# P times V in plain float32, two heads side by side on TensorE's columns

## The chip, the cores and the metric

The kernel runs on one core of one Trainium2 chip. A core has TensorE (PE, matmuls from SBUF into PSUM), VectorE (DVE), ScalarE (ACT), GpSimd (POOL) and a queue of transfers issued by SyncE (SP). The metric is the device time of one execution in microseconds, the median of several runs.

## The reference

Three parts run one behind the other for 4 batches (B), 8 heads (H), 576 tokens (S) and a head size of 64 (D).

```python
scores = scale * np.matmul(q, k.transpose(0, 1, 3, 2))
cum = np.cumsum(np.maximum(s, 0.0), axis=-1)
bias = -(cum[:, :, :, None] - cum[:, :, None, :])
scores = np.where(causal, -1000000000.0, scores + np.minimum(bias, 0.0))
attn = softmax(scores)              # max, exp, sum, divide
x = np.matmul(attn, v)              # "P times V", heads side by side: [B, S, 512]
h = relu(x @ w_in); gate = sigmoid(conv3(h)); x = (h * gate) @ w_out
u = x + (x.T @ U @ V).T
out = u + relu(u @ w_ch1) @ w_ch2
```

The change is in `x = np.matmul(attn, v)`, and in a small part of `scores`.

## The kernel before, in words

The kernel is written as a list of operations, each with an engine, an estimated cost and what it reads and writes. A planner (`Plan.order`) issues them in a simulated order in time: on each engine the operation that is ready and was written first goes first. Eight PSUM banks are given out by class (`sc` for scores, `pt` for transposes, one at a time, `av` for P times V, and so on).

Attention runs over 32 heads, two heads being a pair that shares loads. `att_head(h)` (L1335) writes the scores and the softmax of head `h`, and the transposes and P times V of head `h - 1`. A head's 576 query rows are five blocks: `scores` (L700) makes one block of 128 rows against the keys that the causal mask leaves; `scores4` (L730) makes the last 64 rows of both heads of a pair in one bank, in two halves of 288 keys. DVE adds the mask and takes the maximum, ACT makes the exponentials, POOL divides. `transp` (L775) turns the blocks of P in four groups, and `av` (L809) multiplies: the first half is the queries 0 to 255 (group 0, two steps of widths 256 and 128), the second the queries 256 to 575 (groups 1 to 3, five steps of widths 320, 320, 320, 192 and 64). The steps of a half accumulate in one bank and so keep their order. Every width is a number of queries that stream past a block of 128 keys of V.

There are two forms of arithmetic. In the heads 0 to 7 (`FS` for the scores, `FV` for P times V) the operands are plain float32, and the trace shows two PE instructions for each such matmul. In the heads 8 to 31 each operand is split in a high and a low part of type fp32r (`hi_...` and `lo_...`, L352 to L365), and a product is built from one instruction for each pair of parts that counts. For P times V, V's high and low parts stand side by side in 128 columns (`vv`), P's high and low parts are two tiles (`th` from ACT, `tl` from DVE), and each step is two instructions. The bank then holds two halves of 64 partitions, which ACT and DVE add up (L854, L857).

The first MLP's weights are decoded and split while the first twelve heads run (`load_split`). Its matmuls for one batch (`m1_in` L882, `m1_out` L924) are written between the heads of the next batch, so from head 9 on they fill PE between the steps of attention. When attention ends, its pool in SBUF is closed and the last MLP's weights and activations are put in its place; the second MLP (`m2_in`, `m2_out`) follows.

Of the kernel before, what the change touches and what calls it, by code (L numbers as in the profile page):

```python
# [22 lines left out]
HS = S // 2  # L23
# [2 lines left out]
KT = DM // 128  # L26

FS = range(8)
FV = range(8)

CHUNKS = [512, 512, 512, 512, 256]

# [14 lines left out]

CAPS = dict(sc=3, pt=1, av=5, h=4, y=4, tp=2, t1=4, mh=1, ma=8, my=8, mx=2)

RINGS = dict(P=2, qk=2, th=3, vv=2, qkh=1, x=2, wf=2, xs=5, g=12, hh=3, c=3, x2=4, w64=2, mh=5, o=4, snap=2, tt=3)  # L50


def f32(ap):
# [256 lines left out]
def tile_attention_moe_mixer(  # L310
# [44 lines left out]
    def hi_pool(out, src, r, w, n):  # L355
        pool(n, lambda: nc.gpsimd.tensor_scalar(out(), src(), 1.0, 1.0, ALU.mult, ALU.mult), r, w)
# [230 lines left out]

    def prep_v(h):

        vr = ring(ap, "vr", 1, [128, 2, 5, 64], F32, f"vr{h}")  # L590
        dma(327680, lambda: nc.sync.dma_start(out=vr(), in_=vP[h // 2]), [], [vr])
        for o in range(2):
            if h + o in FV:
                st["v", h + o] = (vr, lambda j, o=o: vr[:, o, j, :])
                continue
            vv = ring(ap, "vv", RINGS["vv"], [128, 5, 128], F32R, f"vv{h + o}")
            hi_pool(lambda vv=vv: vv[:, :, 0:64], lambda o=o: vr[:, o], [vr], [(vv, 0)], 320)
            lo_pool(
                lambda vv=vv: vv[:, :, 64:128],
                lambda o=o: vr[:, o],  # L600
                lambda vv=vv: vv[:, :, 0:64],
                [vr, (vv, 0)],
                [(vv, 1)],
                320,
            )
            st["v", h + o] = (vv, lambda j, vv=vv: vv[:, j, :])

    def prep(h):

# [75 lines left out]
    def products(h, ps, rows, q0, k0, w):  # L685
# [11 lines left out]

        pe(16 + 1.88 * w if h in FS else 2 * mm(w, rows), mms, d["qk"], [ps])

    def scores(h, i):  # L700
        P, sm = st[h]["P"][i], st[h]["sm"]
        w = 128 * i + 128
        ps = bank("sc", f"sc{h}_{i}")
        products(h, ps, 128, 128 * i, 0, w)
        top(ps, 128, w, 384 - 128 * i, lambda: sm[:, i : i + 1], None, [], (sm, f"m{i}"))
        exps(
            lambda: P[:, :w],
            ps,
            128,
            w,  # L710
            lambda: sm[:, i : i + 1],
            lambda: sm[:, 4 + i : 5 + i],
            (sm, f"m{i}"),
            [P, (sm, f"s{i}")],
        )
        if i in RECIP:
            ns = range(max((x + 1 for x in RECIP if x < i), default=0), i + 1)
            ss = [(sm, f"s{n}") for n in ns]
            rs = [(sm, f"r{n}") for n in ns]

            def r():
                return sm[:, 8 + ns[0] : 9 + i]

            dve(2, lambda: nc.vector.tensor_scalar(r(), sm[:, 4 + ns[0] : 5 + i], 1e-9, None, ALU.add), ss, rs)
            dve(15, lambda: nc.vector.reciprocal(r(), r()), rs, rs)  # L725
            for n in ns:
                Pn = st[h]["P"][n]
                normalise(Pn, 128 * n + 128, lambda n=n: sm[:, 8 + n : 9 + n], (sm, f"r{n}"), [Pn])

    def scores4(h):  # L730

        P, sm = st[h]["P"][4], sm4s[h // 2 % 2]
        tiles = []
        for n in range(2):
            ps = bank("sc", f"sc{h}_4_{n}")

            products(h + 1, ps, 128, S - 128, n * HS, HS)
            products(h, ps, 64, S - 64, n * HS, HS)
            top(
                ps,  # L740
                128,
                HS,
                512 * n,
                lambda n=n: sm[:, n : n + 1],
                None if n == 0 else lambda: sm[:, 0:1],
                [] if n == 0 else [(sm, "m0")],
                (sm, f"m{n}"),
            )
            tiles.append(ps)
        for n, ps in enumerate(tiles):  # L750
# [18 lines left out]
        dve(15, lambda: nc.vector.reciprocal(sm[:, 4:5], sm[:, 4:5]), [(sm, "r")], [(sm, "r")])  # L769
        normalise(P, S, lambda: sm[:, 4:5], (sm, "r"), [(P, 0), (P, 1)])  # L770
# [4 lines left out]
    def transp(h, g):  # L775
        d = st[h]
        pt = bank("pt", f"pt{h}_{g}")
        blocks, pos, off, cost = [], {}, 0, 0
        for j, i0, i1 in GROUPS[g]:
            pos[j] = off  # L780
            for i in range(i0, i1 + 1):
                rows = 128 if i < 4 else 64
                blocks.append((j, i, rows, off))
                off += rows
                cost += 109
        n = off

        def tr():


            for j, i, rows, o in reversed(blocks):
                turn = ident[:, 128:256] if i == 4 and h % 2 == 0 else ident[:, 0:128]
                nc.tensor.transpose(
                    pt[:, o + rows - 128 : o + rows], d["P"][i][:, 128 * j : 128 * j + 128], turn
                )

        pe(cost, tr, [ident] + [d["P"][i] for i in sorted({b[1] for b in blocks})], [pt])
        if h in FV:
            th = ring(ap, "th", RINGS["th"], [128, 512], F32, f"tf{h}_{g}")
            hi_act(lambda: th[:, :n], lambda: pt[:, :n], [pt], [th], n)  # L800
            d[f"g{g}"] = ((th,), pos)
            return
        th = ring(ap, "th", RINGS["th"], [128, 512], F32R, f"th{h}_{g}")
        tl = ring(ap, "tl", RINGS["th"], [128, 512], F32R, f"tl{h}_{g}")
        hi_act(lambda: th[:, :n], lambda: pt[:, :n], [pt], [th], n)
        lo_dve(lambda: tl[:, :n], lambda: pt[:, :n], lambda: th[:, :n], [pt, th], [tl], n)
        d[f"g{g}"] = ((th, tl), pos)

    def av(h, half):  # L809
        d = st[h]  # L810
        b, hh = divmod(h, H)
        n, q0, g0 = (256, 0, 0) if half == 0 else (320, 256, 2)
        vb, vof = st["v", h]
# [6 lines left out]
        m = 64 if h in FV else 128  # L820
        tot = len(ops) * m // 64
        c = 0
        for _, g, j, o in ops:
            ts, pos = d[f"g{g}"]
            w = n - o

            def mms(c=c, j=j, o=o, ts=ts, at=pos[j], w=w):
                for k, t in enumerate(ts):
                    nc.tensor.matmul(
                        ps[:m, o:n],  # L830
                        lhsT=vof(j),
                        rhs=t[:, at : at + w],
                        start=c + k == 0,
                        stop=c + k == tot - 1,
                    )

            pe(max(4 * w / 2.4, 160) if h in FV else 2 * mm(w), mms, [vb, *ts], [ps])
            c += len(ts)
        dt = hh // 2
        if hh % 2 == 0 and half == 0:  # L840
            st["x", b, dt] = ring(ap, "x", RINGS["x"], [128, S], F32, f"x{b}_{dt}")
        x = st["x", b, dt]

        def xo():
            return x[a0 : a0 + 64, q0 : q0 + n]

        a0 = 64 * (hh % 2)
        b0 = 64 - a0
        key = (x, (hh % 2, half))
        if h in FV:  # L850
            act(n, lambda: nc.scalar.copy(xo(), ps[0:64, :n]), [ps], [key])
        else:
            tmp = ring(ap, "avt", 1, [128, 320], F32, f"avt{h}_{half}")
            act(n, lambda: nc.scalar.copy(tmp[a0 : a0 + 64, :n], ps[b0 : b0 + 64, :n]), [ps], [tmp])  # L854
            dve(
                n,
                lambda: nc.vector.tensor_tensor(  # L857
                    xo(), ps[a0 : a0 + 64, :n], tmp[a0 : a0 + 64, :n], ALU.add
                ),
                [ps, tmp],  # L860
                [key],
            )
        if hh % 2 == 1 and half == 1:
# [471 lines left out]
    def att_head(h):  # L1335
# [20 lines left out]
            scores(h, 2)  # L1356
        if h > 0:
            transp(h - 1, 1)
            av(h - 1, 0)
        if h < NH:  # L1360
            scores(h, 3)
        if h > 0:
# [1 line left out]
            transp(h - 1, 3)  # L1364
        if h < NH and h % 2 == 0:
            scores4(h)
        if h > 0:
            av(h - 1, 1)

    def mix_parts(b):  # L1370
        def begin():
# [223 lines left out]
```

## Time and profile before

| | |
|---|---|
| median of 3 runs | 849.58 us (849.27 to 849.73) |
| profiled execution, first to last instruction (span) | 847.6 us |
| what the median has beside that span | 2.0 us |
| PE busy | 813.4 us, 96% |
| DVE, ACT, POOL busy | 606.6, 471.0, 392.7 us |
| heads 0 to 7, first MLP weights | to about 77 us |
| heads 8 to 31 with the first MLP | about 77 to 378 us |
| rest of the first MLP, mixing, first layer of the second MLP | about 378 to 647 us |
| second layer of the second MLP | 647 us to the end |

The profiler gives the span of the execution that it took; the time of an execution as the runs measure it is somewhat more than such a span. Matmuls overlap in the records: one is listed for longer than the engine is kept from the next. So start to next start is what a matmul costs.

### The profile page before, as it was taken

To read this page: it belongs to the slowest core of one execution; us is meant where nothing else is said; L and a number is where in the kernel's file an instruction comes from. 1 tells how busy PE (TensorE), PEld (TensorE's weight loads), DVE (VectorE), ACT (ScalarE), POOL (GpSimd) and SP (SyncE) were. 2 spreads that over 40 slices of the span, in tenths; PEclk is the share of its full clock that TensorE was granted. 3 is DMA by queue.
4 is the path that set the end of the run, shared out by engine and by line. 5 is a ranking of instruction groups with operands and counts; after the bars stand their busy time and mean duration, and the time that the engine had idled before them with its cause. 6 is when DMAs were issued, how large, how long until landed. Compare 5 with 4: busy or idle time off the path is not lost. (4 is left out here: it accounts for less than half of the span.)

```text
span 847.6 us, 15619 instructions
## 1 busy us (share of the span) xinstructions
PE 813.4 (96%) x5300; PEld 736.0 (87%) x5300; DVE 606.6 (72%) x1326; ACT 471.0 (56%) x1176; POOL 392.7 (46%) x489
## 2 busy tenths in 40 slices
PE   5989999999999999999997999999999999999998
PEld 3555899999899999999997999999998888888888
DVE  6876999867997589967799989877588732323232
ACT  4887898867877588767675343433344422222211
POOL 3766875864456536447276667555465200000000
PEclk9999999999999999999999999999999999999999
DMA  6666753662455434402134444645368663545443
GB/s 181 185 169 181 197 118 107 161 163 59 129 145 129 115 82 127 129 25 84 56 106 136 156 145 135 205 155 168 128 215 261 194 185 111 176 118 164 127 124 100
DMA packets 66311, 119.71 MB, mean 141 GB/s; under 512 B 9396, under 2 KB 34868, under 8 KB 66232
## 3 DMA queue, kind: packets, MB, share of 16 engines
q1 hardware_dynamic: 66160, 118.70, 48.7%
q8 instruction: 42, 0.69, 0.3%
q14 instruction: 37, 0.30, 0.1%
q10 hardware_dynamic: 72, 0.01, 0.0%
HBM read 68.81 MB, written 28.90 MB: 115 GB/s over the span
## 5 line engine op out<-in xcount | busy, mean ns | idle before, releaser
L1277 PE MATMUL my<-mh,w 128*128 128x512 f32 (+1 forms) x560 | 158.8, 368 | 0.0
L1258 DVE SCALAR_TENSOR_TENSOR ml<-ml,mh 128x512 fp32r<-128x512 f32 (+1 forms) x80 | 53.2, 673 | 104.4 <-ACT mh L1255 104.4
L1178 PE MATMUL ma_S<-u,W 128*128 128x288 f32 x768 | 119.7, 296 | 5.0 <-DVE s L1194 4.9
L935 PE MATMUL y<-gh,w1o 128*128 128x288 f32 x512 | 118.0, 301 | 0.5 <-DVE c L914 0.5
L1255 ACT ACTIVATE mh<-ml 128x512 fp32r<-128x512 f32 (+1 forms) x80 | 46.9, 589 | 127.7 <-DMA ml<-ch_d 68.8
L1277 PEld LDWEIGHTS my<-mh,w 128*128 128x128 f32 x560 | 101.6, 189 | 17.5
L1178 PEld LDWEIGHTS ma_S<-u,W 128*128 128x128 f32 x768 | 107.5, 188 | 7.4 <-DVE s L1194 7.3
L679 POOL TENSOR_SCALAR P<-P,sm 128x128 f32<-128x128 f32 (+3 forms) x128 | 73.4, 592 | 82.6 <-DVE sm L725 76.6
L1277 PE MATMUL my<-ml,w 128*128 128x512 f32 (+1 forms) x280 | 103.0, 368 | 0.0
L1178 PE MATMUL ma_A<-u,W 128*128 128x288 f32 x576 | 92.8, 296 | 1.6 <-ACT p L1190 1.5
L935 PEld LDWEIGHTS y<-gh,w1o 128*128 128x128 f32 x512 | 86.3, 188 | 1.7 <-DVE c L914 1.1
L1178 PEld LDWEIGHTS ma_A<-u,W 128*128 128x128 f32 x576 | 81.9, 188 | 2.7 <-ACT p L1190 2.2
L365 POOL TENSOR_TENSOR gl<-c,gh 128x288 fp32r<-128x288 f32 x64 | 55.5, 870 | 61.8 <-ACT gh L920 58.5
L651 DVE CUSTOM_DVE_ANT_0 sc<-sc,mask 128x128 f32<-128x128 f32 (+2 forms) x144 | 68.6, 495 | 20.7 <-PE sc L690 19.3
L893 PE MATMUL h<-xh,w1h 128*128 128x290 f32 x256 | 80.0, 312 | 1.1 <-DVE c L914 0.7
L893 PE MATMUL h<-xl,w1h 128*128 128x290 f32 x256 | 76.2, 298 | 0.0
L893 PE MATMUL h<-xh,w1l 128*128 128x290 f32 x256 | 76.1, 297 | 0.0
L935 PE MATMUL y<-gl,w1o 128*128 128x288 f32 x256 | 75.0, 293 | 0.0
L668 ACT ACTIVATE P<-sc,sm 128x128 f32<-128x128 f32 (+3 forms) x128 | 67.6, 531 | 11.5 <-DVE sm L651 9.9
L905 DVE SCALAR_TENSOR_TENSOR c<-h,cw,c 128x288 f32<-128x288 f32 x128 | 64.1, 509 | 5.8 <-ACT c L901 4.9
L362 DVE TENSOR_TENSOR tl<-pt,th 128x384 fp32r<-128x384 f32 x96 | 54.5, 567 | 10.8 <-ACT th L353 10.6
L1277 PEld LDWEIGHTS my<-ml,w 128*128 128x128 f32 x280 | 52.8, 189 | 8.7
(147 smaller groups left out, 1989.6 us busy)
## 6 DMA issues: line engine op xcount, KB each, us to landing
ml<-ch_d SPq DMA_DIRECT2D x64, 256.0 KB
ch_d<-p SPq DMA_DIRECT2D x64, 144.0 KB
raw_w<-w_in SPq DMA_DIRECT2D x16, 512.0 KB
raw_w2a<-w_in SPq DMA_DIRECT2D x16, 512.0 KB
raw_w2b<-w_in SPq DMA_DIRECT2D x16, 512.0 KB
t<-qk_in SPq DMA_DIRECT2D x24, 288.0 KB
qkB<-t SPq DMA_DIRECT2D x24, 288.0 KB
qkA<-t SPq DMA_DIRECT2D x24, 288.0 KB
```

The costliest lines, as they stand in the source:

```text
L362: dve(n, lambda: nc.vector.tensor_tensor(out(), src(), f32(hi()), ALU.subtract), r, w)
L365: pool(n, lambda: nc.gpsimd.tensor_tensor(out(), src(), f32(hi()), ALU.subtract), r, w, two=True)
L651: lambda: nc.vector.tensor_tensor_reduce(out=ps[:rows, :w], in0=ps[:rows, :w], in1=mask[:rows, m0 : m0 + w], scale=-0.125, scalar=3.0e38 i ...
L668: lambda: nc.scalar.activation(out(), ps[:rows, :w], ACTF.Exp, bias=low(), scale=-1.0, accum_out=total()),
L679: lambda: nc.gpsimd.tensor_scalar(t[:, :w], t[:, :w], r(), 1.0, ALU.mult, ALU.mult),
L893: nc.tensor.matmul(ps[:, :W], lhsT=ww, rhs=xx, start=kt + n == 0, stop=kt == KT - 1 and n == 2)
L905: lambda k=k: nc.vector.scalar_tensor_tensor(c(), hh[:, k : k + HS], cw[:, 3 * f + k : 3 * f + k + 1], c(), ALU.mult, ALU.add),
L935: nc.tensor.matmul(ps[:, :HS], lhsT=ww, rhs=xx(), start=f + n == 0, stop=f == NF1 - 1 and n == 2)
L1178: nc.tensor.matmul(ps[:, :HS], lhsT=ww, rhs=uu, start=k == 0, stop=k == 5)
L1255: act(n, lambda: nc.scalar.activation(mh[:, :n], raw(), ACTF.Relu), [ml], [mh])
L1258: lambda: nc.vector.scalar_tensor_tensor(ml[:, :n], raw(), 0.0, f32(mh[:, :n]), ALU.max, ALU.subtract),
L1277: nc.tensor.matmul(ys[c][dt][:, :n], lhsT=ww, rhs=xx[:, :n], start=f + k == 0, stop=f == NF2 - 1 and k == 2)
```

## The change

P times V is done in plain float32 in all heads, not only in the first eight. Neither P nor V is split any more: `prep_v` only loads V, and `transp` makes one tile for each group, by ACT. `av` takes a pair of heads at once. One bank of 128 partitions holds both: each step is a float32 matmul of the even head on the array's columns 0-63 and one of the odd head on columns 64-127, written in turns. ACT copies both heads out in one instruction of 128 partitions, and DVE's addition is gone. `av` of a pair is written in the head after the pair's second. The tiles of transposed P have their own buffers for each group and for even and odd heads, and V has two buffers. In the first eight heads the last 64 rows of both heads of a pair are also made as two float32 products on columns 0-63 and 64-127 (`last_rows`).

```diff
-FV = range(8)
-RINGS = dict(P=2, qk=2, th=3, vv=2, ...)
+RINGS = dict(P=2, qk=2, vr=2, ...)
 def prep_v(h):
-        vr = ring(ap, "vr", 1, [128, 2, 5, 64], F32, f"vr{h}")
+        vr = ring(ap, "vr", RINGS["vr"], [128, 2, 5, 64], F32, f"vr{h}")
         dma(327680, lambda: nc.sync.dma_start(out=vr(), in_=vP[h // 2]), [], [vr])
-            hi_pool(lambda vv=vv: vv[:, :, 0:64], ...)
-            lo_pool(lambda vv=vv: vv[:, :, 64:128], ...)
+        st["v", h // 2] = vr
+    def last_rows(h, ps, k0, w):
+        ts = [st[h + o]["qk"][0] for o in range(2)]
+        def mms():
+            for o, t in enumerate(ts):
+                nc.tensor.matmul(
+                    ps[64 * o : 64 * o + 64, :w],
+                    lhsT=t[:, 0, S - 64 : S],
+                    rhs=t[:, 1, k0 : k0 + w],
+                    start=True, stop=True,
+                    tile_position=(0, 64 * o),
+                )
+        pe(16 + 2.7 * w, mms, ts, [ps])
 def scores4(h):
+            if h in FS:
+                last_rows(h, ps, n * HS, HS)
+            else:
                 products(h + 1, ps, 128, S - 128, n * HS, HS)
                 products(h, ps, 64, S - 64, n * HS, HS)
 def transp(h, g):
-        th = ring(ap, "th", RINGS["th"], [128, 512], F32R, f"th{h}_{g}")
-        tl = ring(ap, "tl", RINGS["th"], [128, 512], F32R, f"tl{h}_{g}")
+        th = ring(ap, f"th{h % 2}_{g}", 1 if h % 2 or g > 1 else 2, [128, n], F32, f"th{h}_{g}")
         hi_act(lambda: th[:, :n], lambda: pt[:, :n], [pt], [th], n)
-        lo_dve(lambda: tl[:, :n], lambda: pt[:, :n], lambda: th[:, :n], [pt, th], [tl], n)
 def av(h, half):
+            pairs = [st[h + e][f"g{g}"] for e in range(2)]
+            def mms(c=c, j=j, o=o, w=w, pairs=pairs):
+                for e, (t, pos) in enumerate(pairs):
+                    nc.tensor.matmul(
+                        ps[64 * e : 64 * e + 64, o:n],
+                        lhsT=vr[:, e, j, :],
+                        rhs=t[:, pos[j] : pos[j] + w],
+                        start=c == 0, stop=c == len(ops) - 1,
+                        tile_position=(0, 64 * e),
+                    )
-            pe(max(4 * w / 2.4, 160) if h in FV else 2 * mm(w), mms, [vb, *ts], [ps])
+            pe(max(4 * w / 2.4, 160), mms, [vr, *(t for t, _ in pairs)], [ps])
-            act(n, lambda: nc.scalar.copy(xo(), ps[0:64, :n]), [ps], [key])
-            act(n, lambda: nc.scalar.copy(tmp[a0 : a0 + 64, :n], ps[b0 : b0 + 64, :n]), [ps], [tmp])
-            dve(n, lambda: nc.vector.tensor_tensor(xo(), ps[...], tmp[...], ALU.add), [ps, tmp], [key])
+        act(n, lambda: nc.scalar.copy(x[:, q0 : q0 + n], ps[:, :n]), [ps], [(x, half)])
 def att_head(h):
-            av(h - 1, 0)
+            if h % 2 == 0:
+                av(h - 2, 0)
-        if h > 0:
-            av(h - 1, 1)
+        if h > 0 and h % 2 == 0:
+            av(h - 2, 1)
```

## Rows read from the trace of the kernel before

**Rows 1.** The page, part 1: busy time of each engine, share of the span, instructions.
```profile
PE 813.4 (96%) x5300; PEld 736.0 (87%) x5300; DVE 606.6 (72%) x1326; ACT 471.0 (56%) x1176; POOL 392.7 (46%) x489
```

**Rows 2.** Windows: stretch and length, busy time by engine, PE's clock, DMA share, GB/s.
```profile
17.80:77.30 59.50, 54.48 (x256) 31.60 (x256) 48.38 (x124) 47.35 (x127) 41.94 (x46) 1.00 0.61 172
77.30:378.00 300.70, 295.18 (x2171) 280.58 (x2170) 248.06 (x686) 236.89 (x656) 175.29 (x270) 1.00 0.49 123
```

**Rows 3.** Timeline of PE, a float32 head: start, length, instruction, count.
```profile
60.56 0.86 PE L829 MATMUL av<-tf,vr 128*64 128x256 f32 x4
61.35 0.33 PE L793 MATMUL pt<-ident,p 128*128 128x128 f32 x1
...
61.83 2.27 PE L829 MATMUL av<-tf,vr 128*64 128x320 f32 x10
64.03 0.44 PE L793 MATMUL pt<-ident,P 128*128 128x128 f32 x2
```

**Rows 4.** Timeline of PE, split heads: first and following instruction of three blocks.
```profile
148.49 0.31 PE L829 MATMUL av<-th,vv 128*128 128x320 f32 x1
148.64 0.31 PE L829 MATMUL av<-tl,vv 128*128 128x320 f32 x1
148.78 0.22 PE L690 MATMUL sc<-qkB 128*128 128x128 f32 x1
...
151.04 0.31 PE L829 MATMUL av<-th,vv 128*128 128x320 f32 x1
...
151.71 0.33 PE L793 MATMUL pt<-ident,P 128*128 128x128 f32 x1
...
154.12 0.28 PE L829 MATMUL av<-th,vv 128*128 128x256 f32 x1
...
154.41 0.28 PE L829 MATMUL av<-tl,vv 128*128 128x128 f32 x1
154.52 0.30 PE L690 MATMUL sc<-qkB 128*64 128x288 f32 x1
```

**Rows 5.** Timeline of PE where float32 and split matmuls meet.
```profile
39.06 0.70 PE L690 MATMUL sc<-qkF 128*128 128x256 f32 x2
39.53 0.40 PE L893 MATMUL h<-xh,w1h 128*128 128x290 f32 x1
39.77 0.30 PE L893 MATMUL h<-xl,w1h 128*128 128x290 f32 x1
39.91 0.29 PE L893 MATMUL h<-xh,w1l 128*128 128x290 f32 x1
40.13 0.86 PE L829 MATMUL av<-tf,vr 128*64 128x256 f32 x4
```

**Rows 6.** Timeline of PE, last rows of a float32 pair, then its P times V.
```profile
29.39 2.01 PE L690 MATMUL sc<-qkF 128*64 128x288 f32 x6
31.24 0.43 PE L829 MATMUL av<-tf,vr 128*64 128x320 f32 x1
```

**Rows 7.** Groups of instructions, whole run: count, busy us, mean ns, idle before.
```profile
L362 DVE TENSOR_TENSOR tl<-pt,th 128x384 fp32r<-128x384 f32 x96 | 54.5, 567 | 10.8 <-ACT th L353 10.6
...
L857 DVE TENSOR_TENSOR x<-av,avt 64x256 f32<-64x256 f32 (+1 forms) x48 | 21.7, 452 | 7.6 <-ACT avt L854 4.5 <-POOL xl L365 2.3
L365 POOL TENSOR_TENSOR vv<-vr,vv 128x320 fp32r<-128x320 f32 x24 | 21.5, 896 | 1.3
...
L854 ACT COPY avt<-av 64x256 f32<-64x256 f32 (+1 forms) x48 | 18.9, 394 | 3.9 <-PE av L829 2.9
...
L356 POOL TENSOR_SCALAR vv<-vr 128x320 fp32r<-128x320 f32 x24 | 13.4, 561 | 10.2 <-PE av L829 8.3 <-DMA vr<-vP_in 1.3 <-PE sc L690 0.6
...
L851 ACT COPY x<-av 64x256 f32<-64x256 f32 (+1 forms) x16 | 6.3, 393 | 0.9 <-PE av L829 0.7
```

**Rows 8.** Waits of PE and of its weight loads, 77 to 380 us: total, times, longest.
```profile
PE pt L793 <- ACT P L668: 2.0, 2, 1.0
...
PEld h L893 <- DVE c L914: 1.6, 4, 1.0
```

More of the change, by code (lines that the diff above doesn't have):

```diff
@@ L48 @@
 CAPS = dict(sc=3, pt=1, av=5, h=4, y=4, tp=2, t1=4, mh=1, ma=8, my=8, mx=2)
-RINGS = dict(P=2, qk=2, th=3, vv=2, qkh=1, x=2, wf=2, xs=5, g=12, hh=3, c=3, x2=4, w64=2, mh=5, o=4, snap=2, tt=3)
+RINGS = dict(P=2, qk=2, vr=2, qkh=1, x=2, wf=2, xs=5, g=12, hh=3, c=3, x2=4, w64=2, mh=5, o=4, snap=2, tt=3)
 def f32(ap):
@@ L588, in prep_v @@
     def prep_v(h):
-        vr = ring(ap, "vr", 1, [128, 2, 5, 64], F32, f"vr{h}")
+        vr = ring(ap, "vr", RINGS["vr"], [128, 2, 5, 64], F32, f"vr{h}")
         dma(327680, lambda: nc.sync.dma_start(out=vr(), in_=vP[h // 2]), [], [vr])
[L592 to L606, printed above, removed]
+        st["v", h // 2] = vr
     def prep(h):
@@ L698, in products @@
         pe(16 + 1.88 * w if h in FS else 2 * mm(w, rows), mms, d["qk"], [ps])
+    def last_rows(h, ps, k0, w):
[6 more added lines that the diff above has]
+                    rhs=t[:, 1, k0 : k0 + w],
+                    start=True,
+                    stop=True,
+                    tile_position=(0, 64 * o),
+                )
+        pe(16 + 2.7 * w, mms, ts, [ps])
     def scores(h, i):
@@ L735, in scores4 @@
             ps = bank("sc", f"sc{h}_4_{n}")
-            products(h + 1, ps, 128, S - 128, n * HS, HS)
-            products(h, ps, 64, S - 64, n * HS, HS)
+            if h in FS:
+                last_rows(h, ps, n * HS, HS)
+            else:
+                products(h + 1, ps, 128, S - 128, n * HS, HS)
+                products(h, ps, 64, S - 64, n * HS, HS)
             top(
@@ L797, in transp @@
         pe(cost, tr, [ident] + [d["P"][i] for i in sorted({b[1] for b in blocks})], [pt])
[L798 to L802, printed above, removed]
-        th = ring(ap, "th", RINGS["th"], [128, 512], F32R, f"th{h}_{g}")
-        tl = ring(ap, "tl", RINGS["th"], [128, 512], F32R, f"tl{h}_{g}")
+        th = ring(ap, f"th{h % 2}_{g}", 1 if h % 2 or g > 1 else 2, [128, n], F32, f"th{h}_{g}")
         hi_act(lambda: th[:, :n], lambda: pt[:, :n], [pt], [th], n)
-        lo_dve(lambda: tl[:, :n], lambda: pt[:, :n], lambda: th[:, :n], [pt, th], [tl], n)
-        d[f"g{g}"] = ((th, tl), pos)
+        d[f"g{g}"] = (th, pos)
     def av(h, half):
-        d = st[h]
-        b, hh = divmod(h, H)
+        b, dt = h // H, h % H // 2
         n, q0, g0 = (256, 0, 0) if half == 0 else (320, 256, 2)
-        vb, vof = st["v", h]
+        vr = st["v", h // 2]
         ps = bank("av", f"av{h}_{half}")
@@ L819, in av @@
         ops.sort()
[L820 to L824, printed above, removed]
+        for c, (_, g, j, o) in enumerate(ops):
             w = n - o
-            def mms(c=c, j=j, o=o, ts=ts, at=pos[j], w=w):
-                for k, t in enumerate(ts):
+            pairs = [st[h + e][f"g{g}"] for e in range(2)]
+            def mms(c=c, j=j, o=o, w=w, pairs=pairs):
+                for e, (t, pos) in enumerate(pairs):
@@ L829, in mms @@
                     nc.tensor.matmul(
[L830 to L834, printed above, removed]
-                    )
-            pe(max(4 * w / 2.4, 160) if h in FV else 2 * mm(w), mms, [vb, *ts], [ps])
-            c += len(ts)
-        dt = hh // 2
-        if hh % 2 == 0 and half == 0:
+                        ps[64 * e : 64 * e + 64, o:n],
@@ L841, in av @@
+                        lhsT=vr[:, e, j, :],
+                        rhs=t[:, pos[j] : pos[j] + w],
+                        start=c == 0,
+                        stop=c == len(ops) - 1,
+                        tile_position=(0, 64 * e),
+                    )
+            pe(max(4 * w / 2.4, 160), mms, [vr, *(t for t, _ in pairs)], [ps])
+        if half == 0:
             st["x", b, dt] = ring(ap, "x", RINGS["x"], [128, S], F32, f"x{b}_{dt}")
         x = st["x", b, dt]
-        def xo():
-            return x[a0 : a0 + 64, q0 : q0 + n]
@@ L847, in av @@
[L847 to L850, printed above, removed]
-            act(n, lambda: nc.scalar.copy(xo(), ps[0:64, :n]), [ps], [key])
-        else:
-            tmp = ring(ap, "avt", 1, [128, 320], F32, f"avt{h}_{half}")
-            act(n, lambda: nc.scalar.copy(tmp[a0 : a0 + 64, :n], ps[b0 : b0 + 64, :n]), [ps], [tmp])
[L855 to L862, printed above, removed]
@@ L863, in av @@
-        if hh % 2 == 1 and half == 1:
+        act(n, lambda: nc.scalar.copy(x[:, q0 : q0 + n], ps[:, :n]), [ps], [(x, half)])
+        if half == 1:
             th = ring(xp, "xh", RINGS["xs"], [128, S + 2], F32R, f"xh{b}_{dt}")
```

## The prediction

> **What bounds the kernel now.** I read the page's busy shares first, then the shares by stage, then the order on TensorE in two stages, then the waits. TensorE (PE) is busy for 96% of the span [rows 1], but that is a mean over stages of different work, so the table of stretches decides [rows 2]. The page's chain of waits starts only in the later stages and says nothing of the stage that changes.
>
> - Stage 1, heads 0 to 7 in float32 (17.8 to 77.3 us): PE is busy 54.5 of 59.5 us, but VectorE (DVE) 48.4 and ScalarE (ACT) 47.4. PE leads, with two engines close behind.
> - Stage 2, heads 8 to 31 between the first MLP's matmuls (77.3 to 378 us): PE 295.2 of 300.7 us, DVE 248.1, ACT 236.9, GpSimd (POOL) 175.3. PE is the bound, and 5.5 us is all that its waits hold.
> - The two stages behind it hold nothing of the change. They shift as a block: the space of the attention pool is handed on when attention ends.
>
> So in stage 2 the change is worth what it does to PE's own time; the work it takes from DVE, ACT and POOL is mostly off the path.
>
> **What a head's P times V costs on PE today.** Matmuls overlap in the records, so I take start to next start. In float32 [rows 3] the first half (widths 256 and 128, two instructions each) goes from 60.56 to 61.35, 0.79 us, and the second (320, 320, 320, 192, 64) from 61.83 to 64.03, 2.20 us: 2.99 us a head, 5.98 a pair. Each of the two instructions streams at two cycles of 2.4 GHz a column: 2 x 1600 columns x 2 / 2.4 GHz = 2.67 us, and the rest is the entry to each block. In split form [rows 4] the first half takes 154.12 to 154.52, 0.40; the first 320 148.49 to 148.78, 0.29; the second 320 the same by its form; the last three 151.04 to 151.71, 0.67. That is 1.65 a head, 3.30 a pair.
>
> **The new form.** A pair has seven steps, each of four instructions: head A first and second, head B first and second, A on columns 0-63 and B on 64-127. No row of before shows two matmuls side by side on different columns, so the price is bounded from both sides. With no overlap a pair costs its two heads, 5.98 us. With full overlap it costs one head, 2.99.
>
> I choose near the lower end. A float32 instruction of width 320 takes 0.27 us and a split one of the same width 0.15 [rows 3, 4], so two float32 streams side by side ask for about the data that one split stream already gets, and the halves share no columns and no weights. But starts follow program order in every row. So A's second instruction must start before B's first: A1 runs alone, A2 beside B1, then B2 beside the next step's A1. With T the time of one instruction, a step on its own costs 3T, and n steps in a row 2T each plus one T.
>
> The last steps, in one block: 0.27 + 2 x (3 x 0.267 + 0.16 + 0.053) = 2.29; the first half 0.213 + 2 x 0.32 = 0.85. Sum 3.15 a pair. Where the steps come apart as they do in stage 2 of before (the first half, 320, 320, then three together [rows 4]): 0.85 + 0.80 + 0.80 + 1.23 = 3.68.
>
> To this comes the change of form. In [rows 5] the last float32 scores go from 39.06 to 39.53 for 0.43 us of streaming; the first split matmul behind them then takes 0.24 to the next start and the second 0.14, so leaving float32 costs about 0.14; entering costs 0.08 (39.91 to 40.13 against 0.14). Behind a transpose the entry is paid today as well. I count 0.15 a block: two blocks 0.3, four 0.6.
>
> - Stage 2: a pair goes from 3.30 to between 3.45 and 4.28; twelve pairs, +1.8 to +11.8 us. Other work is always ready there to come between the steps, but steps behind transposes pay nothing extra for entry, so I take +0.45 a pair, **+5.4 us**.
> - Stage 1, P times V: four pairs go from 5.98 to 3.45 to 4.28: PE gets 6.8 to 10.1 us back, say 9.
> - Stage 1, last rows of scores: eight half rows (two for each pair), each with two products of 288 columns, now four instructions in sequence: 4 x 0.24 = 0.96 us by streaming, 1.23 by [rows 6] (six instructions in 1.85 us). In their new form they take 3T = 0.72. Saved 0.24 to 0.5 each, 1.9 to 4 us; I take 3.
>
> So PE is 12 us shorter in stage 1, and 54.5 becomes 42.5. That is under DVE's 48.4, which the change leaves as it is (no float32 head has a low part), and under ACT's 47.4, which loses 8 of 16 copies of 0.39 us [rows 7]: 44.3. DVE's 48.4 is therefore the floor, at most 11.1 us below the 59.5. In that stage P times V also comes in every second head, twice at a time: the heads between leave PE nothing in its place, while the softmax there still needs DVE. I take a little over half of the floor's 11.1: **-6.5 us**, with bounds of -2 (P times V had filled time that the softmax needs anyway) and -11.
>
> **What else is removed.** [Rows 7] price it: 96 subtractions of low parts (54.5 us) and 48 additions (21.7) on DVE, 24 splits of V in two steps on POOL (13.4 + 21.5 us), and on ACT 48 copies (18.9) and 16 (6.3) against 32 new ones; a copy's time goes by its columns, so I price a copy of 128 partitions at the same 0.39, 12.5 us. In stage 2 that takes 76 us from DVE's 248, 35 from POOL's 175 and some 10 from ACT's 237. PE's matmul stream hides nearly all of it: none of these engines had been the bound. What can come back is PE's idle time. Of its waits [rows 8] the largest are on ACT's exponentials and on DVE's gate of the MLP; DVE and ACT, with a shorter queue, answer these sooner. Of 5.5 us I take **-3.5**, bounds 0 and -5.5.
>
> Costs that I set to nothing: the V loads are the same in number and size on SP's queue, and a second buffer only lets them start sooner. The tiles of transposed P now wait for the partner. An odd head has one buffer for each group, so ACT's copy of the next odd head's transposes would stand in front of the exponentials if P times V of the pair before were late; it is due two heads earlier, so I price this at nothing. If that cover were gone each late copy would cost about its length, half a microsecond.
>
> **Sum.** -6.5 + 5.4 - 3.5 = -4.6 us. The profiled execution has a span of 847.6 us; the median of the runs is 849.6, so 2.0 us lie around the span, and I leave them. 847.6 - 4.6 + 2.0 = **845.0 us**, half a per cent faster. With the terms' bounds taken to partly cancel the case runs from 838.5 to 847.9.
>
> **Rivals.**
>
> *No overlap of the columns.* For it: no row shows such overlap. Against it: the data rates above. Stage 1 then gains only on ACT, nothing on PE; stage 2 pays 5.98 - 3.30 = 2.68 a pair, 32.2 us, less the 3.5 of shorter waits: about 878 us.
>
> The Trainium skill bears on this, in "TensorE: Matmul & The Clock Gate", Part 3: it states that several small matmuls placed at different tiles run at the same time, with 2.38 times the speed measured for three column tiles. By that rule this rival falls away; no row here can show it.
>
> *Each change of array width drains PE (the other side).* The rows give it a price: in [rows 6] six float32 instructions that alternate between 128 and 64 columns take 1.85 us for 1.44 of streaming, 0.41 more over three changes, 0.14 a change. Against it: a 64-column product follows a 128-column one at 154.52 in [rows 4] after 0.11 us, no more than the two equal ones before it. Stage 2 would have 12 x 4 blocks with two changes each, 96 x 0.14 = 13.4 us: 845.0 + 13.4 = 858 us. It decides from 4.6 / 96 = 0.05 us a change, where the gain is gone.
>
> The Trainium skill says this in "TensorEngine Tiling (Array Packing)", Key Properties: a change of tiling mode, unlike a change of tile, empties the engine first. [Rows 6] agree and [rows 4] don't, so it holds a chance of its own and not more.
>
> *No change that can be measured.* Stage 1 gives 2 us instead of 6.5, because DVE and the softmax set its pace, and the rest cancels (+5.4 - 3.5 - 2): 849.5 us.
>
> *More than I count.* Steps stay together in stage 2 (+1.8), stage 1 reaches 9, the waits 5: 849.6 - 12.2 = 837.4 us, and less.
>
> **How the numbers follow.** My forecast (838.5 to 847.9) has 0.50; more gain, below that, 0.12; no change 0.12; draining 0.13; no overlap 0.13. A change of 0.2%, 1.7 us, is about what a measurement here can tell from none. Faster is then 0.62, same 0.12, slower 0.26. The range leaves out no overlap (0.13) and the far ends of the others: 834 to 859 us. The likeliest case's own range is 838.5 to 847.9.
>
> **What the profile of after would show.** Right, if B's first instruction starts together with A's second (0.27 us between pairs of starts at width 320), a pair's steps cost 3.2 to 3.7 us of PE, head 8's scores begin about 6 us sooner, and stage 2 is about as long as before with DVE near 172 us. Wrong, if starts within a step are each 0.27 us apart (no overlap), if gaps of 0.1 us and more stand on both sides of each block (draining), or if stage 1 keeps its 59 us with PE waiting for the softmax.

## The result, and the profile after

The changed kernel takes **837.05 us** (median of 4 runs, 835.59 to 837.79); the kernel before took 849.65 us beside it (849.27 to 851.37). The ratio is 0.9845 [0.983, 0.986], so the change is worth 12.6 us. The direction was forecast, the size was not: 845.0 stood for 4.6 us, and the result lies just below the range of 838.5 to 847.9. The rival "more than I count" (837.4 us) came nearest. The profiled execution, the fastest of the four, has a span of 833.8 us, 13.8 below that of before; stages and lines are read from these two.

Page, part 1, of the kernel after, beside [rows 1]:

```profile
PE 797.2 (96%) x5300; PEld 706.9 (85%) x5300; DVE 544.3 (65%) x1182; ACT 453.4 (54%) x1144; POOL 361.7 (43%) x441
```

PE's share is the same 96%: the work and the span shrank together. Windows of the same two stages, beside [rows 2], then the second of them cut at 140 us, after and (the last two lines) before:

```profile
17.80:68.60 50.80, 45.14 (x266) 26.92 (x265) 40.30 (x110) 41.85 (x116) 38.77 (x45) 0.97 0.63 182
68.60:360.80 292.20, 286.10 (x2138) 253.38 (x2137) 192.03 (x552) 222.68 (x631) 145.96 (x222) 0.99 0.51 128
...
68.60:140.00 71.40, 65.30 (x467) 55.16 (x466) 63.32 (x166) 60.62 (x175) 45.67 (x59) 0.98 0.65 165
140.00:360.80 220.80, 220.80 (x1674) 198.21 (x1673) 128.71 (x387) 162.07 (x456) 100.28 (x164) 1.00 0.46 116
```

```profile
77.40:140.00 62.60, 62.12 (x444) 57.04 (x443) 56.43 (x162) 56.58 (x163) 46.49 (x63) 1.00 0.59 155
140.00:377.70 237.70, 232.66 (x1727) 223.14 (x1725) 191.54 (x525) 180.21 (x494) 128.55 (x208) 1.00 0.46 115
```

Two things are to be seen. After 140 us PE has no idle time left (5.0 us before). Ahead of 140 us it is the other way round: 6.1 us idle instead of 0.5, and a mean granted clock of 0.98. The time by stages, from where head 8's first scores, the last P times V and the last stage's first matmuls begin:

| part of the span | before | after | change | forecast |
|---|---|---|---|---|
| stage 1, to head 8's scores | 77.4 | 68.6 | -8.8 | -6.5 |
| stage 2, to the last P times V | 300.3 | 291.9 | -8.4 | +1.9 |
| stage 3, to the second MLP | 269.1 | 272.5 | +3.4 | 0 |
| stage 4 | 200.8 | 200.8 | 0.0 | 0 |

Timeline of PE in the kernel after: both halves of one pair, then a step that came alone, then a half row of last scores:

```profile
141.94 0.87 PE L824 MATMUL av<-th,vr 128*64 128x256 f32 x8
142.74 0.40 PE L675 MATMUL sc<-qkB 128*128 128x288 f32 x1
...
144.76 2.27 PE L824 MATMUL av<-th,vr 128*64 128x320 f32 x20
146.97 0.40 PE L868 MATMUL h<-xh,w1h 128*128 128x290 f32 x1
```

```profile
29.80 0.76 PE L824 MATMUL av<-th,vr 128*64 128x320 f32 x4
30.49 0.33 PE L798 MATMUL pt<-ident,p 128*128 128x128 f32 x1
...
40.98 0.71 PE L691 MATMUL sc<-qkF 128*64 128x288 f32 x4
41.62 0.44 PE L798 MATMUL pt<-ident,P 128*128 128x128 f32 x2
```

Start to next start, a first half takes 0.80 us and a second half 2.21, for **two** heads. One head alone took 0.79 and 2.20 before [rows 3]. The second head is free within a block. A step alone takes 0.69 us: two times the 0.27 of one recorded instruction and 0.15 of entry, not three times. The half row takes 0.64 us; before, six instructions took 1.85 us [rows 6] and a half row has four of them, 1.23.

### The profile page after: what moved, and what is told of

It is laid out like the page before. It is cut to its first block, busy times and chain, and to the rows that moved or that the text cites. A ratio compares the mean times of both kernels' runs of the same rounds, so it can differ in the third digit from the quotient of the medians.

```text
span 833.8 us, 15389 instructions
## 1 busy us (share of the span) xinstructions
PE 797.2 (96%) x5300; PEld 706.9 (85%) x5300; DVE 544.3 (65%) x1182; ACT 453.4 (54%) x1144; POOL 361.7 (43%) x441
## 5 line engine op out<-in xcount | busy, mean ns | idle before, releaser
L664 POOL TENSOR_SCALAR P<-P,sm 128x128 f32<-128x128 f32 (+3 forms) x128 | 75.9, 610 | 86.0 <-DVE sm L727 74.8
L910 PE MATMUL y<-gh,w1o 128*128 128x288 f32 x512 | 112.8, 299 | 0.0
L653 ACT ACTIVATE P<-sc,sm 128x128 f32<-128x128 f32 (+3 forms) x128 | 68.2, 537 | 13.0 <-DVE sm L636 10.2
L352 ACT COPY th<-pt 128x384 f32<-128x384 f32 (+2 forms) x128 | 63.4, 496 | 11.1 <-PE pt L798 9.5
L798 PE MATMUL pt<-ident,P 128*128 128x128 f32 x320 | 60.4, 276 | 1.5 <-POOL P L664 1.5
```

The lines of the kernel that those rows point to most:

```text
L352: act(n, lambda: nc.scalar.copy(out(), src()), r, w)
L653: lambda: nc.scalar.activation(out(), ps[:rows, :w], ACTF.Exp, bias=low(), scale=-1.0, accum_out=total()),
L664: lambda: nc.gpsimd.tensor_scalar(t[:, :w], t[:, :w], r(), 1.0, ALU.mult, ALU.mult),
L798: nc.tensor.transpose(pt[:, o + rows - 128 : o + rows], d["P"][i][:, 128 * j : 128 * j + 128], turn)
L910: nc.tensor.matmul(ps[:, :HS], lhsT=ww, rhs=xx(), start=f + n == 0, stop=f == NF1 - 1 and n == 2)
```

## The experiments

Each kernel is the changed one with the edit shown, if nothing else is said. Ratios are to the kernel before, run on the same chip.

**Without columns of their own.** Both heads on columns 0-63, in two banks, alternating as before:

```diff
-        ps = bank("av", f"av{h}_{half}")
+        pss = [bank("av", f"av{h + e}_{half}") for e in range(2)]
...
-                        ps[64 * e : 64 * e + 64, o:n],
+                        pss[e][0:64, o:n],
...
-                        tile_position=(0, 64 * e),
```

> The kernel after, but both heads of a pair use array columns 0-63 and a bank each; ACT copies each head out by itself (32 more copies of about 0.4 us, off the path). Theory: two column halves run side by side without any loss, so a pair costs PE what one head costs (3.0 us); without it 5.98, sixteen pairs, so PE gets 48 us more, most of it on the path: 875 to 885 us. Rival: the gain comes from the work taken from DVE, POOL and ACT, and the columns matter little: 836 to 843 us.

Measured: 877.82 us, ratio 1.0325 [1.0309, 1.034], 40.8 us above the changed kernel. Timeline of PE, a second half of it:

```profile
156.71 4.33 PE L825 MATMUL av<-th,vr 128*64 128x320 f32 x20
160.97 0.40 PE L869 MATMUL h<-xh,w1h 128*128 128x290 f32 x1
```

The same ten products take 4.26 us instead of 2.21. Without the overlap there is no gain. The rival "no overlap" had priced its kernel at 878 us.

**Head A's steps of a half, then head B's,** each on its own columns:

```diff
-            pe(max(4 * w / 2.4, 160), mms, [vr, *(t for t, _ in pairs)], [ps])
+            todo.append((max(4 * w / 2.4, 160) / 2, mms, [vr, *(t for t, _ in pairs)]))
+        for e in range(2):
+            for cost, mms, rs in todo:
+                pe(cost, lambda mms=mms, e=e: mms(e), rs, [ps])
```

> The kernel after, same columns and bank, but within each half all steps of the even head come first and then all steps of the odd head, instead of in turns. If matmuls start in program order, as the prediction held, the odd head's cannot start beside the even head's: some 45 us more PE work, 875 to 885 us. If each column half has a queue of its own that runs ahead, nothing changes: 835 to 840 us.

Measured: 864.12 us, ratio 1.0147 [1.0118, 1.0175]. Timeline of PE, a first and a second half:

```profile
150.54 0.88 PE L825 MATMUL av<-th,vr 128*64 128x256 f32 x8
151.35 0.44 PE L798 MATMUL pt<-ident,p 128*128 128x128 f32 x2
...
153.32 3.94 PE L825 MATMUL av<-th,vr 128*64 128x320 f32 x20
157.19 0.40 PE L872 MATMUL h<-xh,w1h 128*128 128x290 f32 x1
```

The first half (A's two products, then B's two) still overlaps in full: 0.81 us. Had B's first product waited for A's second to start, it would be 0.43 + 0.43 + 0.21 + 0.15 of entry = 1.22. The second half (five, then five) takes 3.87, near the 4.13 that strict order gives (1.92 until A's last product starts, 2.03 for B's five, 0.18 of entry). In the single records of that block head B's first product starts at 154.99, together with head A's fourth, the one of width 192, so two products of A still stand in front of it. So a product can start ahead of one written before it, but only over a short distance: two products here, not five. The order in turns is what gives the full overlap in the long half.

**Last rows of scores as before.**

```diff
-            if h in FS:
-                last_rows(h, ps, n * HS, HS)
-            else:
-                products(h + 1, ps, 128, S - 128, n * HS, HS)
-                products(h, ps, 64, S - 64, n * HS, HS)
+            products(h + 1, ps, 128, S - 128, n * HS, HS)
+            products(h, ps, 64, S - 64, n * HS, HS)
```

> The kernel after, with the last 64 rows of heads 0 to 7 made as before (128 and 64 columns, one product behind the other). Theory (what the early heads save is given back where the first MLP begins, because the heads arrive there sooner than the DVE work that they need): stage 1 3 to 4 us longer, the whole 0 to 1 us, 837 to 838 us. Rival (PE time saved in stage 1 counts in full): 840 to 841 us.

Measured: 837.89 us, ratio 0.985 [0.9834, 0.9866]: not to be told from the changed kernel. PE's time of the last rows is saved and buys nothing measurable. In the profiles stage 1 is 2.9 us longer and PE has 2.0 us less idle time behind it.

**The new form for heads 0 to 7 alone, and for heads 8 to 31 alone.** The other heads keep the old functions; with the early heads alone, the tiles of transposed P and V have one buffer each, since the split tiles need the space.

```diff
+FV = range(8)
+NEW = range(8)        # the other kernel: range(8, 32)
...
+            if h - 1 not in NEW:
+                av_old(h - 1, 0)
+            elif h % 2 == 0:
                 av(h - 2, 0)
```

> The new form only in heads 0 to 7, with the last rows in two column halves; heads 8 to 31 split as before (the tiles of transposed P have one buffer for each group, V one). Theory (PE time decides, four pairs save 3 us each and the last rows some 4): most of the gain is here: 837 to 842 us. Rival (the gain is the relief of DVE and POOL in heads 8 to 31): 845 to 849 us.

> The new form only in heads 8 to 31; P times V of heads 0 to 7 as before (float32, one head at a time), the last rows in two column halves kept. Theory: twelve pairs save 0.3 us of PE each, the last rows 2 to 4: 842 to 845 us. Rival (relief of DVE, ACT and POOL counts): 839 us or less.

Measured: early heads alone 849.9 us, ratio 0.9995 [0.9984, 1.0005], no gain at all; late heads alone 839.58 us, 0.9875 [0.986, 0.989]. So heads 8 to 31, which the forecast had at +5.4 us of PE less 3.5 of waits, carry 10.3 of the 12.6 us, and the early heads add 2.3. Windows from head 8's scores to 140 us and from there to the last P times V, early heads alone:

```profile
68.30:140.00 71.70, 62.56 (x422) 56.55 (x420) 59.86 (x162) 57.23 (x159) 47.98 (x63) 0.93 0.57 147
140.00:377.80 237.80, 233.84 (x1738) 224.61 (x1736) 193.15 (x533) 182.38 (x500) 130.67 (x210) 1.00 0.45 115
```

Stage 1 does end 9.1 us sooner there. By 140 us that is gone: PE idles 9.1 us instead of 0.5, and a mean clock of 0.93 over 71.7 us costs up to another 5.0. Of the idle time the trace puts 4.8 us to waits that DVE ended and 2.7 to one that a transfer of scores' operands ended; what the single buffers of this kernel cost was not tested apart.

**The removed work put back, outputs unused,** for heads 8 to 31: DVE's subtractions and additions (first two hunks), POOL's two steps on V (the last), or both.

```diff
+        if h >= 8:
+            dve(n, lambda: nc.vector.tensor_tensor(pt[:, :n], pt[:, :n], th[:, :n], ALU.subtract), [pt, th], [pt])
...
+        if h >= 8:
+            for e in range(2):
+                dve(n, lambda: nc.vector.tensor_tensor(ps[0:64, :n], ps[0:64, :n], x[0:64, q0 : q0 + n], ALU.add), [ps, (x, half)], [ps])
...
+        if h >= 8:
+            for o in range(2):
+                pool(320, lambda o=o: nc.gpsimd.tensor_scalar(vr[:, o], vr[:, o], 0.5, 1.0, ALU.mult, ALU.mult), [vr], [vr])
+                pool(320, lambda o=o: nc.gpsimd.tensor_tensor(vr[:, o], vr[:, o], vr[:, o], ALU.add), [vr], [vr], two=True)
```

> The kernel after, with the work that the change takes from DVE and POOL put back in heads 8 to 31, its results used by nobody or without effect (DVE: 96 subtractions on the transposes' bank and 48 additions on the bank of P times V; POOL: V halved and doubled again, two steps a head). Theory: PE's wait time in stage 2 comes back and DVE is again near 250 us of it: 843 to 848 us, about the 849.9 of the run with the early heads alone less the 12 x 0.3 us of PE. Rival (columns are all, relief is nothing): 837 to 839 us.

> The kernel after with only DVE's work put back in heads 8 to 31 (96 subtractions that read and hold the transposes' bank, 48 additions that hold the bank of P times V). All put back gave 848.3. Theory (DVE's 76 us are what the relief is worth): 845 to 848 us. Rival (POOL's work, or ACT's queue): 837 to 840 us.

> The kernel after with only POOL's work put back: V of heads 8 to 31 is halved and doubled again (two steps a head, 35 us in all), and P times V waits for it. If DVE makes the cost of the work put back: 837 to 839 us. If POOL shares it: 840 to 844 us.

Measured: both 848.3 us, ratio 0.998 [0.9966, 0.9994]; DVE's alone 846.44, 0.996 [0.9943, 0.9976]; POOL's alone 840.43, 0.9886 [0.9866, 0.9906]. Of the 12.6 us only 1.9 are left with both put back; DVE's part takes away 9.4 and POOL's 3.4, which lies in the range given for "POOL shares it". Since the added POOL steps work on V in place and P times V waits for them, that run does not tell POOL's time from this wait. Windows cut at 140 us, DVE's work put back:

```profile
69.40:140.00 70.60, 65.44 (x462) 54.99 (x461) 68.00 (x178) 57.86 (x163) 44.52 (x55) 0.98 0.57 147
140.00:371.50 231.50, 227.55 (x1690) 199.83 (x1690) 185.63 (x518) 166.95 (x471) 102.00 (x169) 1.00 0.46 116
```

DVE is busy 68.0 of the first 70.6 us (63.3 of 71.4 in the changed kernel), and behind 140 us PE idles 4.0 us where the changed kernel has none.

The added subtraction holds the one bank of transposes longer. To take that away, DVE worked on copies in SBUF in a further kernel, at the price of one buffer for V instead of two:

```diff
+            tl = ring(ap, "tl", 1, [128, 512], F32, f"tl{h}_{g}")
+            dve(n, lambda: nc.vector.tensor_tensor(tl[:, :n], th[:, :n], th[:, :n], ALU.subtract), [th], [tl])
```

> As the run before this one, but DVE's added work reads SBUF and writes to a spare tile, so that it holds no PSUM bank (V has one buffer, to make room). If the hold on the one transposes' bank makes the cost: 838 to 841 us. If DVE's time makes it: within 2 us of the run before this one.

Measured: 852.34 us, ratio 1.0023 [1.0008, 1.0038], with 17.3 us of idle PE in stage 2. It got slower, not faster, so it doesn't show that the bank was what cost; with V's buffer changed too, it doesn't settle it either. PE's largest waits there ended with a transfer of scores' operands (4.7 us), POOL's division (3.6) and ACT's copy of transposes (3.5).

**The relief alone.** The kernel *before* without DVE's subtractions and additions (the high part of P enters twice, and half of each P times V is not added):

```diff
-        tl = ring(ap, "tl", RINGS["th"], [128, 512], F32R, f"tl{h}_{g}")
...
-        d[f"g{g}"] = ((th, tl), pos)
+        d[f"g{g}"] = ((th, th), pos)
...
+            act(n, lambda: nc.scalar.copy(xo(), ps[b0 : b0 + 64, :n]), [ps], [key])
```

> The kernel before without DVE's subtractions of P's low parts and without its 48 additions (left out: the low part of P, whose tile is replaced by the high part, and one of the two halves of the sum). PE's instructions are those of before. If the relief of DVE is worth what putting it back cost (9 us): 838 to 842 us. If PE's own time is the bound here and only its waits come back: 844 to 847 us.

Measured: 844.41 us, ratio 0.9928 [0.9907, 0.9948], 5.3 us. Windows cut at 140 us:

```profile
77.80:140.00 62.20, 61.28 (x435) 55.80 (x433) 51.11 (x143) 57.05 (x163) 46.23 (x64) 1.00 0.63 161
140.00:370.30 230.30, 229.32 (x1724) 222.21 (x1723) 132.87 (x399) 176.13 (x491) 128.21 (x206) 1.00 0.48 117
```

PE's idle time in stage 2 falls from 5.5 to 1.9 us, by 3.6, where the forecast had -3.5; that it fits so closely is chance, for 3.5 was chosen between 0 and 5.5.

**Is the early gain given back to the decoding of weights?** DVE decodes the first MLP's weights in stage 1, and a shorter stage 1 leaves more of it for stage 2. With the second words of these weights left out, the early heads should gain more, if this were so: once in the changed kernel, once with the late heads alone.

```diff
+        if name.startswith("w1_") and c:
+            def part():
+                return raw().bitcast(F32).rearrange("p (n two) -> p n two", two=2)[:, :n, 1]
+            hi_act(lambda: h[:, :n], part, [raw], [h], n)
+            lo_pool(lambda: l[:, :n], part, lambda: h[:, :n], [raw, h], [l], n)
+            return
```

> The kernel after without DVE's decoding of the first MLP's second weights (eight blocks, three DVE instructions each, some 20 us of DVE between heads 5 and 12, left out; the weights are taken from half of the raw bits). To be read beside the next run, which differs by the early heads alone. Theory: without this DVE work in the way the 8 us that stage 1 saves stay saved: this run 5 to 8 us under the next one. Rival (the gain is lost to something else): 2 to 3 us under it, as 837.05 is under 839.58.

> The run with the new form in heads 8 to 31 only, without DVE's decoding of the first MLP's second weights (left out as in the run before this). Theory: nearly no change against 839.58, since PE has few waits there: 837 to 840 us. Rival: it falls by as much as the run before this one.

Measured: 836.18 us, ratio 0.9835 [0.9816, 0.9855], and 838.26, 0.9855 [0.9841, 0.987]. The early heads are worth 2.1 us with less decoding (14.0 less 11.9, each to its own runs of before) and 2.3 with all of it. This theory of mine falls.

**Fewer early pairs in the old form,** `NEW = range(2, 32)` and `range(4, 32)`:

> The new form from head 2 on; heads 0 and 1 one at a time as before. Theory (early idle time lets the granted clock fall to half): the stretch near 21 us stays at full clock: 836 to 838 us. Rival (what PE saves early counts in full, 3 us a pair): 839 to 840 us.

> The new form from head 4 on; heads 0 to 3 one at a time as before. Theory: what the early pairs save is mostly given back behind head 8, so that two pairs less lose 1 us or gain: 836 to 839 us. Rival: 842 to 843 us.

Measured: 839.49 us (835.72 to 841.15), ratio 0.988 [0.9859, 0.9901], and 841.25 us (839.06 to 845.3), 0.9899 [0.9866, 0.9931]. The first median lies with its rival, the second between theory and rival. Neither differs clearly from the late heads alone, and they don't lie on a line to the changed kernel. Windows around the first pair, changed kernel, then with the first pair old:

```profile
18.00:20.00 2.00, 0.24 (x3) 0.00 (x0) 1.97 (x7) 2.00 (x7) 2.00 (x3) 1.00 0.76 206
20.00:22.00 2.00, 1.83 (x9) 1.56 (x10) 1.44 (x2) 1.16 (x4) 2.00 (x3) 0.70 0.86 257
22.00:24.00 2.00, 2.00 (x7) 1.42 (x6) 2.00 (x2) 0.71 (x3) 1.55 (x2) 0.50 0.54 108
```

```profile
18.00:20.00 2.00, 0.00 (x0) 0.00 (x0) 1.01 (x3) 1.72 (x4) 1.61 (x3) 1.00 1.09 268
20.00:22.00 2.00, 1.53 (x11) 1.24 (x11) 1.04 (x3) 0.89 (x4) 1.47 (x2) 1.00 1.00 200
22.00:24.00 2.00, 2.00 (x11) 1.07 (x10) 1.97 (x5) 2.00 (x7) 0.91 (x2) 1.00 0.74 172
```

An idle stretch of 1.93 us is followed by a granted 0.50 (1.2 GHz) in the one, and a longer one of 2.92 us by an unchanged 1.00 (2.4 GHz) in the other. With the first pair old the lower clock is gone in the profiled execution, yet its span of 833.9 us is no better than 833.8; as the first pair also costs PE more there, this doesn't price the clock.

**Work for PE in its pauses,** to hold the clock up: six small products on the identity beside each of heads 1 to 11.

```diff
+            for i in range(6):
+                wm = bank("wm", f"wm{h}_{i}")
+                def mms(wm=wm):
+                    nc.tensor.matmul(wm[:, :128], lhsT=ident[:, 0:128], rhs=ident[:, 0:128], start=True, stop=True)
+                pe(230, mms, [ident], [wm]).preds.add(start)
```

> The kernel after with 66 added matmuls of 128 columns whose results nobody uses, of the lowest priority, in heads 1 to 11, to keep PE busy where it waits. Theory: the granted clock no longer falls to half in 20 to 100 us (two stretches of 3.4 us in the profile after, 1.7 us each): 833 to 836 us. Rival (the clock doesn't matter, the added work does): 838 to 845 us.

Measured: 870.85 us, ratio 1.0233 [1.0207, 1.0259]. The order that was planned put them in two lumps, as the timeline of PE shows:

```profile
77.85 7.04 PE L1335 MATMUL wm<-ident 128*128 128x128 f32 x26
86.35 15.12 PE L1335 MATMUL wm<-ident 128*128 128x128 f32 x56
```

They hold PE for 22 us, almost in a row, and the clock still fell later, at 116 and 140 us. A miss: it says nothing of what the clock costs.

## Why the prediction was right in direction and wrong in size

**The step that failed: "so a step on its own costs 3T, and n steps in a row 2T each plus one T".** It rested on "starts follow program order in every row" with four instructions a step, A's two ahead of B's two. The rows of after show 2T for a step alone (0.69 us with its entry) and one head's time for a pair: 0.80 + 2.21 = 3.01, the lower bound of 2.99 that the forecast had worked out and not taken. In the kernel's program a float32 product is one instruction; the two are records of the profile, and two records of A and two of B lie side by side. The second experiment shows the rule itself to be too strict here. In stage 2 all blocks of P times V together, each from its start to the next start, take 49.00 us in 98 blocks before and 41.35 in 41 blocks after; the transposes straight ahead of such blocks hold PE for 4.86 us in 24 places instead of 1.58 in 26. The term was +5.4 and measured -7.65 + 3.28 = -4.4. Of that, 2.7 is P times V of heads 6 and 7 (5.99 to 3.31), which falls behind the start of stage 2 and which the forecast had in stage 1; the twelve late pairs come to -1.7.

**The old form was priced too low as well.** The forecast's 3.30 us a pair rests on one block of each kind [rows 4], and its first half follows scores. The 24 late heads take 43.0 us in 94 blocks, 3.58 a pair: 15 of 23 first halves stand behind a transpose and take 0.49 to 0.60 instead of 0.40, as this one of 0.51 in the kernel before, and a single step takes 0.32 on the mean instead of 0.29:

```profile
145.11 0.38 PE L793 MATMUL pt<-ident,P 128*128 128x128 f32 x2
145.44 0.39 PE L829 MATMUL av<-th,vv 128*128 128x256 f32 x1
...
145.95 0.45 PE L690 MATMUL sc<-qkB 128*128 128x512 f32 x1
```

With the transposes straight ahead, a late pair goes from 3.66 to 3.52 us instead of from 3.30 to 3.75. So in the late heads the new form is hardly cheaper for PE than the old one; without the overlap it would be far dearer.

**Breaking up: right. Entry: right inside a block, missed around it.** The forecast had 0.15 us a block and two to four blocks a pair; measured are 0.15 to 0.18 (2.21 less 2.03 of streaming) and 41 / 13 = 3.2 blocks. But "steps behind transposes pay nothing extra for entry" is wrong, and the edge is not one of form. Timeline of PE in the kernel after:

```profile
61.32 0.38 PE L798 MATMUL pt<-ident,P 128*128 128x128 f32 x2
61.63 0.87 PE L824 MATMUL av<-th,vr 128*64 128x256 f32 x8
62.43 0.44 PE L798 MATMUL pt<-ident,p 128*128 128x128 f32 x2
62.71 0.38 PE L798 MATMUL pt<-ident,P 128*128 128x128 f32 x2
...
63.87 0.38 PE L798 MATMUL pt<-ident,P 128*128 128x128 f32 x2
64.09 0.60 PE L675 MATMUL sc<-qkF 128*128 128x256 f32 x2
```

Two transposes take 0.22 us to the next start ahead of float32 scores of 128 columns, 0.31 ahead of float32 products of 64 columns, and 0.28 behind them. So a float32 block of 64 columns costs 0.09 ahead of it, 0.16 inside and 0.06 behind, some 0.15 for each of its two changes of width.

**The rivals on PE.** "No overlap" is out. "Draining" had the price right, 0.14 a change from [rows 6], and such gaps do stand on both sides of each float32 block of 64 columns; at 0.15, 82 changes are some 12 us. It is its total, 858 us, that is out, since it came on top of an overlap priced too small and an old form priced too low. For the split form [rows 4] show no such gap, as the prediction says. The Trainium skill ("TensorE: Matmul & The Clock Gate", Part 3) says that matmuls on different tiles run at once: 2.21 against 4.26 us agree. The Trainium skill says in the same part that matmuls start strictly in order; the first half of the second experiment, 0.81 us where that order gives 1.22, does not agree, and the measurement decides.

**Stage 1: sized too small, its floor wrong.** -6.5 became -8.8. "DVE's 48.4 is therefore the floor" took the stage's DVE work as fixed. After, DVE is busy 40.3 us there: of the weights' decoding, 25 and 12 instructions of its two kinds before, 19 and 10 are left in the stage, the rest came later. Work that only fills a stage is no floor of it.

**The relief: right alone, wrong as a term to be added.** Alone it gives back 3.6 us of idle time, and 5.3 in all; in the changed kernel stage 2 has 0.6 us more idle time than before. But early heads alone give 0, overlap with the removed work put back 1.9, and all together 12.6. The two need each other. Sooner early heads bring the softmax of heads 8 and on to an earlier time, beside the same loads and decoding, and DVE had 19.44 and 19.35 us of work in each 20 us there. Windows of the kernel before:

```profile
100.00:120.00 20.00, 19.79 (x145) 18.84 (x144) 19.44 (x55) 18.63 (x55) 15.67 (x21) 1.00 0.40 114
120.00:140.00 20.00, 20.00 (x155) 19.78 (x155) 19.35 (x58) 18.72 (x55) 13.58 (x19) 1.00 0.48 122
```

The forecast read "off the path" from DVE's 248 of 300.7 us, the mean of the stage. The cut at 140 us shows the limit that this mean hides. In the changed kernel the relief wipes out the 5.0 us of idle time behind 140 us; ahead of it 5.6 us of new idle time come in, and up to 1.7 us of clock. Of the 8.8 us that stage 1 gains, up to 7.3 are given back by 140 us. What is left, 1.5 us or more, is near the early heads' 2.3. Windows of the changed kernel where it happens:

```profile
84.00:88.00 4.00, 2.12 (x14) 1.52 (x12) 4.00 (x7) 2.31 (x6) 2.66 (x3) 1.00 0.89 268
88.00:92.00 4.00, 3.23 (x16) 2.88 (x17) 3.56 (x10) 4.00 (x14) 1.75 (x4) 0.63 1.03 214
92.00:96.00 4.00, 4.00 (x32) 3.50 (x30) 3.54 (x13) 4.00 (x12) 2.78 (x4) 0.94 1.05 216
```

PE is busy 2.12 of 4 us while DVE is busy throughout; then the clock is 0.63 and 0.94, which loses at most 0.37 x 4 + 0.06 x 4 = 1.7 us. The longest of these pauses can be followed back; lines of DVE, ACT and PE there:

```profile
83.26 3.59 DVE L361 TENSOR_TENSOR t<-t,t 128x576 fp32r<-128x576 f32 x2
86.77 0.55 DVE L636 CUSTOM_DVE_ANT_0 sc<-sc,mask 128x384 f32<-128x384 f32 x1
87.47 0.58 ACT L653 ACTIVATE P<-sc,sm 128x384 f32<-128x384 f32 x1 [1.69 <-DVE sm L636]
88.20 0.33 PE L798 MATMUL pt<-ident,p 128*128 128x128 f32 x1 [1.38 <-ACT P L653]
```

DVE splits a pair's queries and keys for 3.6 us before it takes up the mask; ACT waits 1.69 us for the mask and PE 1.38 us for ACT. Most of PE's other waits ahead of 140 us end with ACT's exponentials or POOL, and DVE ends only 0.8 us of them itself.

**"The two stages behind it shift as a block": not quite.** Stage 3 is 3.4 us longer. 1063 matmuls of the first MLP are recorded ahead of attention's end before and 1039 after; 24 at 0.135 us are 3.2 us that only move from stage 2 to stage 3. Nine more (12 recorded ahead of head 8's scores after, 3 before) move to stage 1. Each matmul taken from its start to the next, less idle time, stage 2 changes by -7.65 in P times V, +3.2 in the transposes, -3.8 in the first MLP (33 matmuls less are -4.5; the rest fits the lower clock), +0.6 of idle time and -0.8 in all else: -8.5, measured -8.4.

**Waits and copies.** Waits of PE in stage 2, beside [rows 8], and ACT's copy of both heads, beside [rows 7]:

```profile
PE pt L798 <- ACT P L653: 1.6, 2, 1.4
PE h L868 <- ACT P L653: 1.2, 2, 0.9
...
L837 ACT COPY x<-av 128x256 f32<-128x256 f32 (+1 forms) x32 | 12.9, 402 | 5.6 <-PE av L824 5.6
```

The copy was priced at 0.39 us, 12.5 in all, and takes 0.40 and 12.9. No wait for an odd head's tile of transposes is among PE's, as assumed.

**What stays open.** Putting DVE's work back adds 10.2 us to stage 2, of which 3.0 are idle time, 2.0 moved matmuls and 1.4 P times V; the other 3.8 are longer steps of the remaining matmuls, 2.2 of it in the first MLP, and why is not shown. That DVE at its limit is what eats the early gain follows from the windows, from the one pause followed back and from the put-back work, but the put-back work also holds banks, and the one kernel that should have freed them went the wrong way. What the lower clock alone costs was not measured: the fillers failed, and the kernel without it differs in its first pair too.

## What to carry to other kernels

Two float32 streams of 64 columns each, issued in turns, cost one of them, and every change between such a block and products of 128 columns some 0.15 us, so keep the blocks long; give the halves of the array to two heads in turns, not one head after the other. Where a stage's mean says that an engine has room, cut the stage before calling its work free: the removed DVE work was hidden by the mean, and put back it took away three quarters of the gain. Gains of two edits are not to be added when one brings work forward into a time in which the other's engine is full; run each alone and both.

## What the runs showed of the hardware

- One float32 product is recorded as two matmuls, and two products on columns 0-63 and 64-127 run side by side in full (0.80 and 2.21 us for two heads, 0.79 and 2.20 for one).
- A product on free columns starts ahead of one written before it when two products stand in front (0.81 us), but not over five (3.87).
- Float32 products of 64 columns cost some 0.15 us at each change from or to 128 columns (two transposes take 0.31 us ahead of them and 0.28 behind, 0.22 ahead of float32 products of 128 columns); split products of 64 columns show no such cost [rows 4].
- The granted clock fell to 0.50 after 1.9 us of idle PE at 18 us in one kernel and stayed at 1.00 after 2.9 us in another. It had not fallen in attention in the kernel before.
